# One transpose of 128x32 for the maxima's rows, and the mixer's weights cast on GpSimd from unit 16 on

## The chip, the cores and the metric

The kernel runs on one core of a Trainium2 chip, as one program with one launch. The metric is the device time of one execution in microseconds (us), as the median of several executions; lower is better. The engines of the core are named as in the profile: PE is TensorE (PEld its weight loads), DVE is VectorE, ACT is ScalarE, POOL is GpSimd and SP is SyncE, which here only issues DMAs. Each engine takes its own instructions strictly in the order in which they stand; engines wait for each other by semaphores.

## The reference

All data are float32. The output is `x + s * g`: `s` is full attention with 32 heads of 16 channels over 2048 tokens, `g` is the gate of a token-mixing MLP, and both read the same normalized input.

```python
xn = layernorm(x)                                   # (2048, 512)
# s: attention
q, k, v = split(xn @ wqkv)                          # 32 heads, 16 channels each
p = softmax(einsum("qd,kd->qk", q, k) * 16 ** -0.5) # per head, 2048 x 2048
s = concat(p @ v) @ wo
# g: mixer, the MLP runs over the token axis
u = gelu(einsum("sd,sf->df", layernorm(xn), w1) + b1)   # F = 1792
g = silu(einsum("df,fs->ds", u, w2) + b2).T
out = x + s * g
```

## The kernel before

**Numbers.** A float32 product is made of float32r products: an operand is split into an upper part (a cast to float32r) and a lower part (the rest), and three products are added. `w_split(n)` does that for unit `n` of the mixer's weights, a quarter of a block of 128 columns (512 values a partition): line 179 or 181 casts `raw` to `wh`, on POOL or on ACT, and the helper `sub` (line 107) makes `wl` on POOL. Which engine casts hangs on `steady[0]`, which is set when the loop reaches step 22 (`LEAD`).

**The softmax** is made without a second pass: for each row of queries the maximum of the scores is found first (`max_of`: a score matmul on 48 rows of `q` and `k`, line 537, and a DVE reduction of 128x512, line 541). The negated maxima are then written into two extra rows of the tile `qs[p]` (rows 48 and 49 of each of the two heads in it, upper and lower part), opposite two rows of ones in `ks[p]`. So the second score matmul (`score`, 50 rows, line 1000) gives the score less its maximum, and ACT only has to take the exponential (line 1005). `values` (line 1015) multiplies it with `v`; 32 columns of it are the ones that sum the denominators.

**The main loop** (line 1279) runs over `s` in pairs of steps. A pair has 8 maxima (for the future), 8 scores (22 steps behind), 8 matmuls of `values`, and as many half products of the mixer as a plan by due times gives it (0 to 6, `count`). The order within a pair is written out by hand in strings (`MIDST`). The first 11 pairs, here called the lead, have maxima and the mixer's first products alone; the steady stage follows; the ending (line 1333, strings `ENDING`) has no maxima any more.

**The rows of the maxima.** Sixteen steps of maxima (1024 queries of two heads) make a group; there are 32. At the end of a group, `max_rows` hands out small pieces of work; `piece()` takes one at two places of each pair (all at once in the lead and at the beginning of the ending). Before the change there are five: the reduction to `neg` (128 x 16 values used of 128 x 32), four DVE transposes of 32x32 that each turn one block of 32 partitions into columns of `f` (32 x 128), and with the last of these the cast and the split to `m` on POOL and four DMAs on POOL's own queue, each of which brings eight rows of 128 values into one row of `qs[p]`. The first scores that read these rows stand three pairs after the pair in which the second piece is taken.

**Queues.** All other loads and stores stand on SP, in program order: the mixer's weights (`raw`, three buffers, line 170), the stores of the mixer's inner result (`u_d`), the loads of `q`, `k` and `v`, and at the end the loads and stores of the output's parts. SP's DMAs use eight semaphores in turn, and each waits until the one eight before it has landed.

Of the kernel before, what the change touches and what calls it, by code (L numbers as in the profile page):

```python
# [8 lines left out]
F32 = mybir.dt.float32  # L9
F32R = mybir.dt.float32r  # L10
# [11 lines left out]
def tile_attention_token_mixer(ctx, tc, x, wqkv, wo, w1, b1, w2, b2, out):  # L22
    nc = tc.nc
    P = 128
# [13 lines left out]
    N_BEFORE = 4  # L38
    scale = DH ** -0.5

    def pool(name, bufs, **kw):
        return ctx.enter_context(tc.tile_pool(name=name, bufs=bufs, **kw))
# [63 lines left out]
    def sub(eng, o, a, b):  # L106
        eng.tensor_tensor(out=o, in0=a, in1=b.bitcast(F32), op=OP.subtract)  # L107

    def move(dst, src, queue=nc.sync):

        queue.dma_start(dst.bitcast(F32), src.bitcast(F32))
# [7 lines left out]
    qs, ks, vps = {}, {}, {}  # L119
# [35 lines left out]
    steady = [False]  # L155
# [16 lines left out]
    def w_split(n):  # L172
        if n >= N_W:
            return
        m = quarters[n][2] - quarters[n][1] if n < N_MIX else 4
        whs[n] = wp.tile([P, 4, P], F32R, name="wh")
        wls[n] = wp.tile([P, 4, P], F32R, name="wl")
        if steady[0]:
            nc.gpsimd.tensor_copy(whs[n][:, :m, :], raws[n][:, :m, :])  # L179
        else:  # L180
            nc.scalar.copy(whs[n][:, :m, :], raws[n][:, :m, :])  # L181
        sub(nc.gpsimd, wls[n][:, :m, :], raws[n][:, :m, :], whs[n][:, :m, :])


    with (
# [230 lines left out]
        for c in range(NC):  # L416
# [18 lines left out]
            for n, (part, g) in enumerate(order):  # L435
                m = slice(g * P, (g + 1) * P)
                ps = bank()
                for w, z in ((wh, 0), (wh, 1), (wl, 0)):
                    for kd in range(ND):
                        nc.tensor.matmul(  # L440
                            ps, w[part][:, kd, m], xt[kd][:, z, :],
                            start=w is wh and z == 0 and kd == 0, stop=w is wl and kd == ND - 1,
                        )
                sg = pst.tile([P, 2, 512], F32R, name="sg")
                nc.scalar.copy(sg[:, 0, :], ps)
                sub(nc.vector, sg[:, 1, :], ps, sg[:, 0, :])
                dst = (q_d, k_d)[part][g]
                move(dst[:, :, cs], sg)
                for f in todo[n * per : min((n + 1) * per, cut)]:
                    f()  # L450
                if c == NC - 1 and n == ND - 1:
                    place_qk(0)
                if c == NC - 1 and n == ND:
                    load_qk(0)
                if c == NC - 2 and n == 0:
                    for i in range(3):
                        w_load(i)
                if c == NC - 2 and n == ND:
                    w_split(0)
                    w_load(3)  # L460
                    w_split(1)
                    w_load(4)
                    w_split(2)
# [43 lines left out]
    sm = pool("sm", 2, reuse_waits="tile")  # L507
# [35 lines left out]
    def max_rows(u):  # L543

        p, r = divmod(u // 2, NB)
        span = r // 8
        neg = negs[u // 16 % 2]
        f = sm.tile([32, P], F32, name="f", bufs=1)


        def turned(c):
            nc.vector.transpose(f[:, 32 * c : 32 * c + 32], neg[32 * c : 32 * c + 32, :])  # L552

        def first_():
            nc.vector.tensor_reduce(
                neg[:, :16].rearrange("p (a b) -> p a b", a=2), mxp.pop(u // 16), axis=AX.X, op=OP.max, negate=True,
            )

        def last():
            turned(3)  # L560
            m = sm.tile([16, 2, P], F32R, name="m", bufs=1)
            nc.gpsimd.tensor_copy(m[:, 0, :], f[:16, :])  # L562
            sub(nc.gpsimd, m[:, 1, :], f[:16, :], m[:, 0, :])
            for a in range(2):
                for t in range(2):
                    row = 64 * a + 48 + t
                    move(
                        qs[p][row : row + 1, span * 1024 : (span + 1) * 1024],
                        m[8 * a : 8 * a + 8, t, :], nc.gpsimd,
                    )  # L570

        return first_, *(lambda c=c: turned(c) for c in range(3)), last

# [703 lines left out]
    for s in range(0, total + 1, 2):  # L1279
        t = s - LEAD  # L1280
# [11 lines left out]
        if s < NU and t >= 0:  # L1292
            steady[0] = True
            some = halves(count(s))
            n = len(some)
            of = BEGIN if begun else END if ended[0] else MIDST
            begun = ended[0]
            n = min(x for x in MIDST if x >= n)
# [34 lines left out]
        elif t < NT:  # L1333
# [6 lines left out]
            while any(strings):  # L1340
                for a in range(2):
                    c = strings[a].pop(0) if strings[a] else ""
# [19 lines left out]
        if s < NU and s % 16 == 14:  # L1362
            pieces.extend(max_rows(s + 1))
            piece()
# [5 lines left out]
        if 0 <= t < NT:  # L1370
            p, r = divmod(t, SPP)
# [48 lines left out]
    for k0, kn in parts_:  # L1420
        at = slice(k0 * P, (k0 + kn) * P)
# [53 lines left out]
```

## Time and profile before

| | us |
|---|---|
| median of 3 runs (1633.03 to 1633.38) | 1633.11 |
| the profiled execution | 1634.06 |
| its span, first to last instruction | 1632.2 |
| PE busy in the span | 1621.9 |
| DVE busy | 1418.1 |
| ACT busy | 1194.5 |
| POOL busy | 575.4 |

The lead's first maximum is reduced at 148.7 us, the first score matmul comes at 203 us, the last maximum at 1565 us. A group of the steady stage takes some 44.5 us. A matmul's time is from its start to its modelled end, and two matmuls that use different halves of the rows overlap; so a busy PE may still start its matmuls later than it could, and the distance from start to start is what to look at. Rows of SP are issues of DMAs, not transfers.

### The profile page before, as it was taken

How to read it: one execution, taken by the hardware profiler on the slowest of the kernel's cores; microseconds unless marked ns; L12 is line 12 of the kernel's file. 1: busy time of each engine (PE TensorE's matmuls, PEld its weight loads, DVE VectorE, ACT ScalarE, POOL GpSimd, SP SyncE). 2: the span in 40 equal slices, each digit the busy share in tenths (PEclk: the TensorE clock that was granted, in tenths of full speed). 3: DMA queues.
4: the chain of work that ended last, by engine and by line, in shares of the span. 5: the costliest groups of instructions: out<-in, count | busy, mean ns of one | idle time of the engine just before them, and what ended most of it. 6: DMA issues, size and time to landing. Idle time of an engine off the chain costs nothing.

```text
span 1632.2 us, 31813 instructions
## 1 busy us (share of the span) xinstructions
PE 1621.9 (99%) x11948; PEld 892.0 (55%) x11948; DVE 1418.1 (87%) x2506; ACT 1194.5 (73%) x2297; POOL 575.4 (35%) x676
## 2 busy tenths in 40 slices
PE   9999999999999999999999999999999999999998
PEld 7888845555554545555555545555554545544554
DVE  7655989999999999999999999999999999999955
ACT  4333488777877777787777777787777777788785
POOL 0223743333443334332433223223222332662434
PEclk9999999999999999999999999999999999999999
DMA  6479621415133141836150522305152515354344
GB/s 226 174 247 227 122 59 47 82 34 95 41 53 76 38 79 35 191 121 111 37 85 18 99 57 46 70 30 77 37 85 59 91 37 78 100 110 134 117 151 168
DMA packets 150775, 152.89 MB, mean 94 GB/s; under 512 B 51340, under 2 KB 109708, under 8 KB 147548
## 3 DMA queue, kind: packets, MB, share of 16 engines
q1 hardware_dynamic: 146044, 149.70, 38.8%
q8 instruction: 94, 1.54, 0.4%
q0 software_dynamic: 4288, 0.62, 0.3%
q14 instruction: 61, 0.50, 0.1%
q10 hardware_dynamic: 288, 0.52, 0.1%
HBM read 99.63 MB, written 50.32 MB: 92 GB/s over the span
## 4 chain that ended last, share of the span: by engine, by line
PE 98%; DVE 1%; ACT 0%; DMA 0%; SPq 0%; issue 0%; DVEq 0%; ACTq 0%
PE av L1015 31%; PE sc L1165 16%; PE sc L1000 10%; PE sc L537 8%; PE mx L1000 8%; PE mx L1165 7%; PE mx L537 6%; PE sc L440 3%; PE mx L440 2%; PE mx L1112 1%; PE sc L1112 1%; PE sc L1215 1%; PE av L440 1%; PE sc L116 1%; PE sc L114 1%; PE sc L115 1%
## 5 line engine op out<-in xcount | busy, mean ns | idle before, releaser
L541 DVE TENSOR_REDUCE mxp<-sc 128x1 f32<-128x512 f32 x1129 | 735.9, 681 | 74.7 <-PE sc L537 49.7
L1005 ACT ACTIVATE prob<-sc 128x512 f32<-128x512 f32 x1135 | 638.3, 604 | 168.8 <-PE sc L1000 98.2
L541 DVE TENSOR_REDUCE mxp<-mx 128x1 f32<-128x512 f32 x919 | 606.0, 681 | 50.3 <-PE mx L537 30.9
L1005 ACT ACTIVATE prob<-mx 128x512 f32<-128x512 f32 x913 | 523.1, 606 | 127.3 <-PE mx L1000 71.7
L1015 PE MATMUL av<-prob,vp 128*32 128x512 f32 x4096 | 543.0, 604 | 0.0
L537 PE MATMUL sc<-big 48*128 48x512 f32 x1129 | 427.8, 417 | 0.0
L1000 PE MATMUL sc<-big 50*128 50x512 f32 x1135 | 423.1, 417 | 0.2 <-ACT prob L1005 0.2
L1165 PE MATMUL sc<-hu,wh 64*128 64x512 f32 x1072 | 359.3, 404 | 0.0
L537 PE MATMUL mx<-big 48*128 48x512 f32 x919 | 349.9, 416 | 0.1
L1000 PE MATMUL mx<-big 50*128 50x512 f32 x913 | 346.9, 415 | 0.5 <-ACT prob L1005 0.5
L1000 PEld LDWEIGHTS sc<-big 50*128 50x128 f32 x1135 | 198.2, 185 | 137.9 <-DVE mxp L541 102.0
L537 PEld LDWEIGHTS sc<-big 48*128 48x128 f32 x1129 | 196.9, 185 | 81.7 <-ACT prob L1005 53.5
L1165 PEld LDWEIGHTS sc<-hu,wh 64*128 64x128 f32 x1072 | 193.9, 184 | 58.8 <-issue 41.9
L1000 PEld LDWEIGHTS mx<-big 50*128 50x128 f32 x913 | 162.2, 185 | 107.4 <-DVE mxp L541 83.3
L1165 PE MATMUL sc<-hu,wl 64*128 64x512 f32 x536 | 215.1, 401 | 0.0
L537 PEld LDWEIGHTS mx<-big 48*128 48x128 f32 x919 | 160.9, 185 | 74.4 <-ACT prob L1005 38.1
L1015 PEld LDWEIGHTS av<-prob,vp 128*32 128x32 f32 x4096 | 81.8, 108 | 171.8 <-issue 161.4
L1165 PE MATMUL mx<-hu,wh 64*128 64x512 f32 x464 | 156.2, 405 | 0.0
L179 POOL CAST wh<-raw 128x512 fp32r<-128x512 f32 (+1 forms) x105 | 61.3, 584 | 255.2 <-PE sc L537 57.7
L107 POOL TENSOR_TENSOR wl<-raw,wh 128x512 fp32r<-128x512 f32 (+1 forms) x113 | 136.6, 1210 | 28.9 <-ACT wh L181 20.4
L562 POOL CAST m<-f 16x128 fp32r<-16x128 f32 x32 | 9.0, 280 | 311.2 <-DVE f L552 308.4
L1165 PEld LDWEIGHTS sc<-hu,wl 64*128 64x128 f32 x536 | 98.8, 184 | 13.3 <-issue 5.9
(240 smaller groups left out, 1592.0 us busy)
## 6 DMA issues: line engine op xcount, KB each, us to landing
raw<-in_B_w_dram SPq DMA_DIRECT2D x93, 256.0 KB
big<-k_d SPq DMA_DIRECT2D x96, 128.0 KB
big<-q_d SPq DMA_DIRECT2D x96, 128.0 KB
q_d<-sg SPq DMA_DIRECT2D x16, 512.0 KB
k_d<-sg SPq DMA_DIRECT2D x16, 512.0 KB
num_d<-ev SPq DMA_DIRECT2D x30, 256.0 KB
u_d<-uo SPq DMA_DIRECT2D x14, 512.0 KB
hu<-u_d SPq DMA_DIRECT2D x14, 512.0 KB
```

What stands on the lines that cost most here:

```text
L107: eng.tensor_tensor(out=o, in0=a, in1=b.bitcast(F32), op=OP.subtract)
L114: nc.tensor.matmul(ps, wh, mh, start=first, stop=False)
L115: nc.tensor.matmul(ps, wh, ml, start=False, stop=False)
L179: nc.gpsimd.tensor_copy(whs[n][:, :m, :], raws[n][:, :m, :])
L440: nc.tensor.matmul(ps, w[part][:, kd, m], xt[kd][:, z, :], start=w is wh and z == 0 and kd == 0, stop=w is wl and kd == ND - 1,)
L537: nc.tensor.matmul(ps, q[o : o + 48, r * P : (r + 1) * P], k[o : o + 48, c * 512 : (c + 1) * 512], start=True, stop=True,)
L541: return nc.vector.tensor_reduce(mxp[u // 16][:, a, r % 8, c : c + 1], ps, axis=AX.X, op=OP.max)
L1000: nc.tensor.matmul(ps, ks[p][o : o + 50, kb * P : (kb + 1) * P], qs[p][o : o + 50, at : at + 512], start=True, stop=True,)
L1005: return nc.scalar.activation(e, ps, AF.Exp, scale=scale)
L1015: nc.tensor.matmul(av[32 * j : 32 * j + 32, :], vps[p][:, kbs[c], 16 * a : 16 * a + 32], prob.pop((t, a, c)), start=first, stop=last,)
L1112: nc.tensor.matmul(ps(a), w(r), m(r), start=first, stop=last)
L1165: i = nc.tensor.matmul(ps(), w(r), m(r), start=first and first_half, stop=last and not first_half)
```

## The change

The four transposes become one of 128x32. DVE turns every block of 32x32 in its own partitions, so `f` is now 128 x 32: block `b` of the maxima stays on partitions 32b to 32b+31. `m` is cast and split in this layout (32 values a partition on 128 partitions, before 128 values on 16). A row of `qs[p]` is then gathered from four blocks: four DMAs for each row, 16 in all, each of 8 pieces of 32 values, and they are issued by SP. The group's pieces are now two, so the second, with transpose, cast, split and DMAs, is taken at the place where the first of the four transposes was. Apart from that, `w_split` casts units from 16 on, three of which fall before `steady[0]` is set, on POOL.

```diff
-        if steady[0]:
+        if steady[0] or n >= 4 * N_BEFORE:
             nc.gpsimd.tensor_copy(whs[n][:, :m, :], raws[n][:, :m, :])
         else:
             nc.scalar.copy(whs[n][:, :m, :], raws[n][:, :m, :])
@@ max_rows
-        f = sm.tile([32, P], F32, name="f", bufs=1)
-        def turned(c):
-            nc.vector.transpose(f[:, 32 * c : 32 * c + 32], neg[32 * c : 32 * c + 32, :])
+        f = sm.tile([P, 32], F32, name="f", bufs=1)
...
         def last():
-            turned(3)
-            m = sm.tile([16, 2, P], F32R, name="m", bufs=1)
-            nc.gpsimd.tensor_copy(m[:, 0, :], f[:16, :])
-            sub(nc.gpsimd, m[:, 1, :], f[:16, :], m[:, 0, :])
+            nc.vector.transpose(f, neg)
+            m = sm.tile([P, 2, 32], F32R, name="m", bufs=1)
+            nc.gpsimd.tensor_copy(m[:, 0, :], f)
+            sub(nc.gpsimd, m[:, 1, :], f, m[:, 0, :])
             for a in range(2):
                 for t in range(2):
                     row = 64 * a + 48 + t
-                    move(
-                        qs[p][row : row + 1, span * 1024 : (span + 1) * 1024],
-                        m[8 * a : 8 * a + 8, t, :], nc.gpsimd,
-                    )
-        return first_, *(lambda c=c: turned(c) for c in range(3)), last
+                    to = qs[p][row : row + 1, span * 1024 : (span + 1) * 1024]
+                    to = to.rearrange("o (r g b) -> o r g b", r=8, g=4)
+                    for g in range(4):
+                        at = 32 * g + 8 * a
+                        move(to[:, :, g, :], m[at : at + 8, t, :], nc.sync)
+        return first_, last
```

SP at the end of the lead, before; `u_d` is the store of a mixer block, `raw` a load of weights:

```order
L170 DMA prob<-in_B_w_dram 128x4x128 x2
L111 DMA u_d_104<-uo 128x1024
L170 DMA raw<-in_B_w_dram 128x4x128 x3
L111 DMA u_d_105<-uo 128x1024
L170 DMA raw<-in_B_w_dram 128x4x128 x2
L145 DMA vp<-v_d 128x16x48
```

And now:

```order
L170 DMA prob<-in_B_w_dram 128x4x128 x2
L111 DMA u_d_104<-uo 128x1024
L111 DMA big<-m 1x8x32 x16
L170 DMA raw<-in_B_w_dram 128x4x128 x3
L111 DMA u_d_105<-uo 128x1024
L170 DMA raw<-in_B_w_dram 128x4x128 x2
```

The first group's 16 DMAs stand ahead of the three loads that bring units 16 to 18.

POOL at the same place, from the split of unit 16 on, before:

```order
L107 TENSOR_TENSOR wl<-raw,wh 128x512
L675 TENSOR_TENSOR sq<-sq,u 128x512
L107 TENSOR_TENSOR wl<-raw,wh 128x512
L630 TENSOR_TENSOR u<-u,sq 128x512
L631 TENSOR_TENSOR sq<-u 128x512
L632 TENSOR_SCALAR sq<-sq 128x512
L633 TENSOR_TENSOR sq<-sq,u 128x512
L107 TENSOR_TENSOR wl<-raw,wh 128x512
L678 TENSOR_TENSOR t<-t,u 128x512
```

And now (line numbers are 3 lower):

```order
L179 CAST wh<-raw 128x512
L107 TENSOR_TENSOR wl<-raw,wh 128x512
L672 TENSOR_TENSOR sq<-sq,u 128x512
L179 CAST wh<-raw 128x512
L107 TENSOR_TENSOR wl<-raw,wh 128x512
L627 TENSOR_TENSOR u<-u,sq 128x512
L628 TENSOR_TENSOR sq<-u 128x512
L629 TENSOR_SCALAR sq<-sq 128x512
L630 TENSOR_TENSOR sq<-sq,u 128x512
L179 CAST wh<-raw 128x512
L107 TENSOR_TENSOR wl<-raw,wh 128x512
L675 TENSOR_TENSOR t<-t,u 128x512
```

Three casts were put in ahead of their splits; ACT loses the same three.

SP at the beginning of the ending, now; `u`, `sq`, `xt` and `gt` are buffers for the output's parts (lines 952 and 954 before). Before the change the last two rows below followed directly on `gt`:

```order
L949 DMA u<-g_d 128x512
L951 DMA sq<-y_d 128x512
L949 DMA xt<-g_d 128x512
L951 DMA gt<-y_d 128x512
L111 DMA big<-m 1x8x32 x16
L941 DMA big<-in_A_x_dram 128x512
L927 DMA y_d<-t 128x512
```

The last group's rows stand behind the eight loads that the ending begins with; before they stood on POOL, ahead of the gate's products (lines 922 and 923).

## The prediction

> **What bounds the kernel now.** I read first the busy times and the chain of work that ended last, then DVE's largest groups, then three stretches of one steady group by windows.
>
> ```profile
> PE 1621.9 (99%) x11948; PEld 892.0 (55%) x11948; DVE 1418.1 (87%) x2506; ACT 1194.5 (73%) x2297; POOL 575.4 (35%) x676
> ...
> PE 98%; DVE 1%; ACT 0%; DMA 0%; SPq 0%; issue 0%; DVEq 0%; ACTq 0%
> ...
> L541 DVE TENSOR_REDUCE mxp<-sc 128x1 f32<-128x512 f32 x1129 | 735.9, 681 | 74.7 <-PE sc L537 49.7
> ...
> L541 DVE TENSOR_REDUCE mxp<-mx 128x1 f32<-128x512 f32 x919 | 606.0, 681 | 50.3 <-PE mx L537 30.9
> ```
>
> The chain runs through PE for 98% of the span. DVE, which the change relieves, is well loaded, but in front of its reductions it stood idle for 74.7 + 50.3 = 125 us, most of it until a maximum's matmul was done: an engine that set the pace would not wait so. PE's own 99% says little, since its ends are modelled. So I ask whether PE starts its matmuls more slowly while the transposes run. One group: the reduction to `neg` at 945.43, the four transposes from 946.76 to 954.40, DVE's first idle time ahead of 958.02 (columns of the first rows below: the stretch and its length, then busy us and count by engine).
>
> ```profile
> core 0: us, PE busy (x) PEld busy (x) DVE busy (x) ACT busy (x) POOL busy (x), PEclk, DMA share, GB/s
> 945.30:958.00 12.70, 12.70 (x99) 6.32 (x98) 11.92 (x24) 9.04 (x18) 3.24 (x7) 1.00 0.22 64
> 958.00:972.00 14.00, 14.00 (x110) 7.06 (x108) 12.59 (x21) 10.81 (x21) 3.49 (x5) 1.00 0.16 49
> 972.00:989.70 17.70, 17.70 (x138) 9.22 (x134) 15.94 (x26) 14.73 (x30) 5.58 (x6) 1.00 0.15 46
> ...
> 945.43 0.22 DVE L555 TENSOR_REDUCE neg<-mxp 128x16 f32<-128x64 f32 x1
> ...
> 946.76 0.19 DVE L552 STREAM_TRANSPOSE f<-neg 32x32 f32<-32x32 f32 x1
> ...
> 954.40 0.20 DVE L552 STREAM_TRANSPOSE f<-neg 32x32 f32<-32x32 f32 x1
> ...
> 958.02 1.29 DVE L541 TENSOR_REDUCE mxp<-sc 128x1 f32<-128x512 f32 x2 [0.44 <-PE mx L1165]
> ```
>
> With the transposes PE starts 99/12.70 = 7.80 matmuls per us, without them 110/14.00 = 7.86 and 138/17.70 = 7.80. DVE's share goes from 94% to 90%, and PE hardly notices. PE bounds the steady stage.
>
> **Term 1, DVE in the steady stage.** Three transposes fall away in each of 30 steady groups; the one that stays handles four blocks side by side.
>
> ```profile
> L552 DVE STREAM_TRANSPOSE f<-neg x128: 187/199/204, 188.3 to 1567.5; 32x32 f32<-32x32 f32 x128
> ```
>
> No row shows a transpose of 128x32. Between 0.2 us (one 32x32, if partitions work in parallel) and 0.8 us (four of them), I take 0.2, since other rows of DVE with 128 partitions go by elements per partition. DVE saves 3 x 0.199 = 0.6 us in a group. What reaches PE: had the first stretch run at the rate of the two others together (248/31.70 = 7.82), its 99 matmuls had taken 12.66 us, 0.04 less. Times 30 that is 1.3 us for the whole of neg and transposes (0.22 + 0.80 us of DVE), of which 0.6 us, some 60%, goes: **-0.8 us**. Bounds: 0 (nothing arrives, or the transpose takes 0.8) and -3 (the stretch's loss is twice as large and more, as far as one group can mislead). That all of it arrives is a rival below.
>
> **Term 2, the lead.** Two small gaps of PE stand there.
>
> ```profile
> 188.33 0.84 DVE L552 STREAM_TRANSPOSE f<-neg 32x32 f32<-32x32 f32 x4
> ...
> 189.96 0.39 PE L537 MATMUL sc<-big 48*128 48x512 f32 x1
> 190.40 0.50 PE L537 MATMUL mx<-big 48*128 48x512 f32 x1
> ...
> 204.08 0.63 ACT L181 CAST wh<-raw 128x512 fp32r<-128x512 f32 x1
> ...
> 205.26 0.50 PE L1000 MATMUL mx<-big 50*128 50x512 f32 x1 [0.52 <-ACT prob L1005]
> ```
>
> From 189.96 to 190.40 PE starts nothing for 0.44 us, where it else starts a matmul every 0.23 or so: 0.2 us that DVE's four transposes in a row cost, as I read it. At 205.26 PE waited 0.52 us for an exponential; ahead of the first ones stands the cast of unit 18, which delays them by about 0.5 us and now is POOL's. Both gone: **-0.6 us** (0 to -0.7).
>
> **Term 3, POOL at the end of the lead.** POOL receives three casts and loses four DMAs a group.
>
> ```profile
> L107 POOL TENSOR_TENSOR wl<-raw,wh 128x512 fp32r<-128x512 f32 x97 | 124.9, 1288 | 27.6 <-ACT wh L181 20.4
> L111 POOL DMA_DIRECT2D big<-m x128 | 66.2, 530 | 2.6 <-PE sc L1215 2.6
> L179 POOL CAST wh<-raw 128x512 fp32r<-128x512 f32 x89 | 54.9, 617 | 246.5 <-PE sc L537 56.8 <-PE mx L1000 48.2 <-PE mx L537 47.4
> ...
> 185.06 2.08 SPq L170 DMA_DIRECT2D raw<-in_B_w_dram  x3
> ...
> 965.80 1.09 SPq L730 DMA_DIRECT2D d<-ev  x2
> ...
> 1555.46 0.69 SPq L784 DMA_DIRECT2D uo<-rec_d  x1
> 1562.46 1.28 POOL L791 TENSOR_TENSOR u<-u,uo 96x512 f32<-96x512 f32 x1 [4.89 <-DMA uo<-rec_d]
> ```
>
> The casts cost 3 x 0.62 = 1.9 us, the DMAs of a group 4 x 0.53 = 2.1 us; POOL is ahead, were it not for SP. The loads of units 16 to 18 went out at 185.06; now the 16 small DMAs stand before them, and these wait for `m` (transposed from 188.33, cast and split in some 0.5 us: 189.1). An issue of a small DMA that gathers 256-byte pieces takes 1.09/2 = 0.55 us, the large ones that follow each other 0.43 to 0.47 apart; I take 0.5, bounds 0.34 and 0.55. So the burst takes 8 us, and the loads go out at 197.1 instead of 185.06. Their landing on SP is in no row of mine; between 1.6 us (4 KB on POOL's queue) and 7.0 us (a 512 KB broadcast, 1555.46 to 1562.46) I take 4: unit 16 lands at 201.1, is cast and split by 203.0.
>
> ```profile
> 209.92 1.32 POOL L678 TENSOR_TENSOR t<-t,u 128x512 f32<-128x512 f32 x1
> ...
> 213.04 0.63 ACT L668 CAST uo<-t 128x512 fp32r<-128x512 f32 x1
> ...
> 203.27 0.39 PE L1165 MATMUL sc<-hu,wl 64*128 64x512 f32 x1
> ```
>
> PE's first product with that `wl` stood at 203.27: just in time. Behind it, POOL has ten more instructions up to `t`, now about 10.8 us without a gap, so `t` ends near 213.8 instead of 211.24, and ACT, which is 0.5 us ahead of 213.04 without its cast, waits some 1.3 us with exponentials behind. PE has seven banks and ACT slack of its own: **+0.5 us** (0, if loads land in 2 us; 2.5 if in 6).
>
> **Term 4, the steady rows and the last ones.** In the steady stage the rows must be in place for the score three pairs later.
>
> ```profile
> 955.44 2.08 POOL L111 DMA_DIRECT2D big<-m  x4
> ...
> 960.62 0.19 PEld L1000 LDWEIGHTS sc<-big 50*128 50x128 f32 x1
> ...
> DMA to landing us min/median/max: 1.5/1.6/4.5
> ```
>
> Before: last issue at 957.0, landing 1.6 later, use at 960.62: 2 us to spare. Now `m` is ready at 947.5, the burst lasts until 955.5, lands at 957.1: 3.5 us to spare. SP is held at this place until `m` is there, so loads that it took early now go out with the burst's end; weights are loaded two units (some 25 us) ahead, which covers it: 0.
>
> The ending has less.
>
> ```profile
> 1567.76 0.28 POOL L562 CAST m<-f 16x128 fp32r<-16x128 f32 x1 [2.77 <-DVE one L1227]
> 1568.12 0.52 POOL L107 TENSOR_TENSOR m<-f,m 16x128 fp32r<-16x128 f32 x1
> 1571.27 2.04 POOL L111 DMA_DIRECT2D big<-m  x4 [2.63 <-PE sc L1215]
> 1573.32 1.30 POOL L922 TENSOR_TENSOR t<-t,gt 128x512 f32<-128x512 f32 x1
> 1574.69 1.29 POOL L923 TENSOR_TENSOR t<-t,xt 128x512 f32<-128x512 f32 x1
> ...
> 1570.33 0.32 SPq L954 DMA_DIRECT2D sq<-y_d  x1
> 1576.01 0.32 SPq L952 DMA_DIRECT2D xt<-g_d  x1
> 1576.38 0.42 SPq L954 DMA_DIRECT2D gt<-y_d  x1
> ...
> 1578.80 0.50 PE L1000 MATMUL mx<-big 50*128 50x512 f32 x1
> ```
>
> The rows' first use is at 1578.80. The burst stands behind `xt` and `gt`, and `xt` waits for POOL's L923 (1575.98 before). Without its DMAs POOL comes to L922 at 1567.8 and ends L923 at 1570.4; so SP issues `xt` and `gt` until 1571.25, then the burst. Its last DMA goes out 15 x 0.5 later, 1578.75, lands 1.6 later at 1580.4: PE stands for **+1.6 us**. Bounds: 0 (issues of 0.34: landing at 1577.9) and +5.2 (0.55 and a landing of 4.5 behind the 256 KB loads: 1584.0). PE is the chain there, nothing takes it back.
>
> The Trainium skill, "DMA: Bandwidth & Descriptors", section "Anatomy of one DMA — SWDGE (gpsimd) path", gives a DMA a fixed cost of about 2.0 us; this trace has 1.6 for the nearest, so the measurement is used. By the page the estimate of this stall would be 2.0 and the sum +1.1.
>
> **Sum**: -0.8 - 0.6 + 0.5 + 1.6 = +0.7 us. On the profiled execution (1634.06; span 1632.2 and 1.9 around it) that is 1634.8; this execution lay 0.95 above the median of the runs, 1633.11, so the predicted median is **1633.8**.
>
> **Rivals.** *DVE sets the pace around each group's end.* For it: DVE is 94% busy in 945.3 to 958. Then all of 3 x 0.199 x 30 = 17.9 us arrives, 1615; a quarter of it, 4.5 us, gives 1629.4 with the other terms. Against it: the even rates of PE and DVE's 125 us of idle. 0.14 for a gain over 0.2%.
> *SP's burst decides, slower.* Place: the ending, where eight loads of 256 KB go ahead of it. From landing at 1578.8 on each us counts one for one; at the upper bounds +5.2, with the lead's 2.5 and nothing gained about 1641, typically 1638. For it: `xt` did wait 5.7 us here. Should an issue take over 0.72 us, the steady rows come late too (947.5 + 16 x 0.72 + 1.6 = 960.6), and 0.8 would cost 30 x 1.3 = 39 us, 1672; SP's rows are all against that. Together 0.22.
> The Trainium skill, same page, section "Specifications", speaks against pieces under 512 bytes (read-modify-write); here they are 128, before 512. No row prices it.
> *The wide transpose costs as much as four.* Then term 1 and 0.2 of term 2 fall away: +1.7, 1634.8; 0.06, no change either. My forecast has 0.58.
>
> **The numbers.** A measurement of this kernel tells about 0.2% (3.3 us) from no change: faster is under 1629.8, slower over 1636.4. Faster 0.14, same 0.58 + 0.06 = 0.64, slower 0.22. Range: terms at their low ends with the first rival's edge give 1629.4, with the second rival's typical 1638: 1629 to 1638.5.
>
> **What would show it.** Term 1: a transpose of 0.2 us, DVE's idle ahead of L541 up by about the 18 us saved, with PE's steady rate unchanged. Term 2: no wait near 205 us. Term 3: units 16 to 18 loaded near 197 us, POOL's `wl` near 203. Term 4: 16 issues of 0.5 us on SP, and in the ending PE held at its first score of the last group. Wrong it would be if steady groups became shorter than 44.4 us, or if the ending showed no gap.

## The result, and the profile after

| | before | after |
|---|---|---|
| median, us | 1633.24 (1633.03 to 1634.18, 4 runs) | 1656.40 (1654.44 to 1659.94, 4 runs) |
| the profiled execution, us | 1634.06 | 1654.44 |
| its span, us | 1632.2 | 1652.7 |

The ratio is 1.0143, 95% interval 1.0125 to 1.0161. The change makes the kernel 23 us slower; 1633.8 was predicted, and the range ended at 1638.5. The profiled execution lies 2.0 us under the median, so the traces have 20.4 of the 23 us to account for.

From the page of the profile after: the busy times, the chain by engine, DVE's two largest groups (busy, mean ns of one, idle before them).

```profile
PE 1627.6 (98%) x11948; PEld 891.6 (54%) x11948; DVE 1407.9 (85%) x2410; ACT 1194.0 (72%) x2294; POOL 505.0 (31%) x551
...
PE 89%; DMA 4%; SPq 3%; POOL 2%; DVE 1%; issue 1%; ACT 0%; DVEq 0%; POOLq 0%
...
L541 DVE TENSOR_REDUCE mxp<-sc 128x1 f32<-128x512 f32 x1129 | 739.2, 684 | 90.0 <-PE sc L537 60.6
...
L541 DVE TENSOR_REDUCE mxp<-mx 128x1 f32<-128x512 f32 x919 | 608.4, 684 | 61.1 <-PE mx L537 37.2
```

And from the groups by line and form, the transposes:

```profile
L556 DVE STREAM_TRANSPOSE f<-neg 128x32 f32<-128x32 f32 x32 | 6.5, 202 | 0.1
```

The transposes did what was asked of them: 25.3 us of DVE became 6.5, and DVE's idle time ahead of its reductions rose from 125 to 151 us. New is the chain: it ran through PE for 98% of the span, now for 89%. The rest goes through DMAs, SP's queue and POOL.

The waits of PE that the change brought (total us, times, longest):

```profile
PE mx L997 <- DMA big<-m: 8.2, 3, 5.7
...
PE sc L997 <- DMA big<-m: 3.7, 2, 2.4
PE sc L997 <- ACT prob L1002: 2.2, 1, 2.2
```

And the 512 DMAs with the rows of the maxima, from the view of the tile `m` (duration of an issue in ns: least, median, most; first and last start):

```profile
L111 SPq DMA_DIRECT2D big<-m x512: 634/635/798, 188.4 to 1595.6; - x171
```

An issue takes 0.635 us (the median). The places themselves, from the timeline after (start, length, engine, what; in brackets what was waited for and how long): SP's burst, then the first score that reads its rows. In order of time: the end of the lead, groups 11 and 16, then group 17 as an ordinary one (the weight load is that of its first score), groups 24, 27 (burst alone) and 28, the ending.

```profile
188.36 11.12 SPq L111 DMA_DIRECT2D big<-m  x16
199.53 1.54 SPq L170 DMA_DIRECT2D raw<-in_B_w_dram  x3
...
202.70 0.61 POOL L179 CAST wh<-raw 128x512 fp32r<-128x512 f32 x1 [6.14 <-DMA raw<-in_B_w_dram]
203.37 0.50 PE L1162 MATMUL sc<-hu,wh 64*128 64x512 f32 x1 [1.03 <-POOL wh L179]
...
685.28 11.00 SPq L111 DMA_DIRECT2D big<-m  x16
...
697.66 0.47 PE L997 MATMUL mx<-big 50*128 50x512 f32 x1 [1.46 <-DMA big<-m]
...
906.36 13.60 SPq L111 DMA_DIRECT2D big<-m  x16
...
921.33 0.46 PE L997 MATMUL mx<-big 50*128 50x512 f32 x1 [1.04 <-DMA big<-m]
...
952.44 11.00 SPq L111 DMA_DIRECT2D big<-m  x16
...
965.79 0.19 PEld L997 LDWEIGHTS sc<-big 50*128 50x128 f32 x1
...
1263.37 13.90 SPq L111 DMA_DIRECT2D big<-m  x16
...
1278.53 0.46 PE L997 MATMUL sc<-big 50*128 50x512 f32 x1 [1.24 <-DMA big<-m]
...
1398.98 11.00 SPq L111 DMA_DIRECT2D big<-m  x16
...
1447.02 11.08 SPq L111 DMA_DIRECT2D big<-m  x16
...
1459.59 0.76 PE L997 MATMUL sc<-big 50*128 50x512 f32 x1 [2.44 <-DMA big<-m]
...
1584.85 11.37 SPq L111 DMA_DIRECT2D big<-m  x16
...
1597.49 0.76 PE L997 MATMUL mx<-big 50*128 50x512 f32 x1 [5.66 <-DMA big<-m]
```

Sixteen issues take 11.0 us, 0.69 from start to start. In the ordinary group the last one starts 0.635 us before the burst's end, at 962.8, and a landing takes 1.67 us (next fence); so the rows are there at 964.5, 1.3 us before their first use at 965.79. At four of the 30 steady groups (11, 16, 24 and 28) and in the ending the burst starts late or is held up within itself, and this 1.3 us is not enough.

Why it is late there, from the chain of the groups at 906 and at 1447:

```profile
905.20 8.65 DMA raw<-in_B_w_dram
...
913.88 0.63 SPq L111
...
919.32 1.67 DMA big<-m
...
921.33 0.46 PE mx L997
...
1414.56 12.71 DMA raw<-in_A_wo_dram
...
1446.83 0.15 POOL m L558
```

At 906 the burst stops halfway: SP's DMAs use eight semaphores in turn, and one of the 16 had to wait until a 256 KB load, issued at 905.20, was in place. Group 24's burst of 13.9 us stands behind the same sequence of loads. At 1447 it is `m` that is late: the burst of group 27 (1398.98 to 1409.99) put off six loads of 256 and 512 KB and, behind them, a block of the output weights; that was issued at 1414.56 and took 12.71 us to land, POOL stood for it, and POOL's products that it delayed stand ahead of `m`. At 685 SP itself was late, with large loads still to issue when `m` was ready (682.3); in the ending its burst began 4.1 us behind `m` (1580.75) for the same reason.

A long wait cost more than itself. Windows of the trace after: behind the end of group 28's wait and right after that, then the same for the ending (columns as in the prediction; PEclk is the granted clock of TensorE as a share of full speed).

```profile
core 0: us, PE busy (x) PEld busy (x) DVE busy (x) ACT busy (x) POOL busy (x), PEclk, DMA share, GB/s
1459.60:1465.60 6.00, 6.00 (x27) 2.05 (x27) 2.29 (x4) 2.77 (x5) 0.00 (x0) 0.50 0.72 229
1466.00:1472.00 6.00, 6.00 (x48) 3.15 (x46) 4.88 (x8) 4.62 (x9) 2.57 (x2) 1.00 0.55 115
1597.50:1602.10 4.60, 4.60 (x21) 2.68 (x25) 0.12 (x2) 3.81 (x8) 0.00 (x0) 0.50 0.58 168
1602.50:1607.10 4.60, 4.60 (x38) 2.24 (x34) 1.66 (x7) 3.26 (x7) 0.00 (x0) 1.00 0.27 101
```

In these two waits (2.44 and 5.66 us) the granted clock fell to 0.50 and stayed there for 6.8 us, and PE got through 27 matmuls in 6.0 us, where it then did 48. With the waits of 1.0 to 2.2 us elsewhere in this trace it stayed at 1.00. By the starts of the same matmuls in the traces before and after, group 28 lost 2.8 us in the wait and 2.8 more under the low clock, the ending 6.2 and 1.8: 4.6 us of the 20.4 come from the clock. No run varies the clock alone, but in the traces of all runs here it fell, while PE still had work, only in or just behind a wait of 1.6 us or more, and with every wait of 2.4 us or more.

To see how much each stretch lost, I compare the starts of the same instruction in two traces: the difference is taken at the first reduction of pair 7 (before the first rows), of pair 16 (behind the lead's end), of the last pair, and at the end of the span. For all kernels of this study, in us against the profile before:

| kernel | up to pair 7 | lead's end, pairs 7 to 16 | steady, pair 16 to last | ending | span |
|---|---|---|---|---|---|
| the change | -0.5 | +2.9 | +9.8 | +8.1 | +20.4 |
| rows on POOL | -0.8 | +3.1 | -0.9 | +1.3 | +2.7 |
| cast alone | -0.8 | -0.5 | -0.4 | 0.0 | -1.6 |
| rows alone | +0.4 | +1.4 | +12.7 | +7.8 | +22.3 |
| four on SP | -0.1 | 0.0 | -0.8 | +0.8 | -0.1 |
| shared queues | +0.7 | -0.9 | -1.1 | +6.2 | +4.9 |
| some groups on POOL | +0.3 | +3.1 | +7.4 | +3.9 | +14.6 |
| twenty on SP, repeated | -0.5 | +11.4 | +256.6 | +15.4 | +282.8 |
| double transposes | -0.4 | +1.0 | +12.6 | 0.0 | +13.2 |
| shared, last as before | -1.0 | -0.9 | -0.9 | -0.6 | -3.4 |
| half dose of transposes | 0.0 | +0.5 | +1.5 | 0.0 | +2.0 |
| shared in six groups | -0.4 | -0.9 | -1.0 | +2.1 | -0.2 |
| four spare on SP | -0.3 | +6.9 | +58.0 | +9.5 | +74.0 |

The first column is scatter, since nothing is changed up to there: up to 1 us between two executions. So a difference of less than 1 us elsewhere in this table proves nothing by itself.

### The profile page after: what moved, and what is told of

Its sections match the earlier page's. It is cut to its first block, busy times and chain, and to the rows that moved or that the text cites. A ratio compares the mean times of both kernels' runs of the same rounds, so it can differ in the third digit from the quotient of the medians.

```text
span 1652.7 us, 32191 instructions
## 1 busy us (share of the span) xinstructions
PE 1627.6 (98%) x11948; PEld 891.6 (54%) x11948; DVE 1407.9 (85%) x2410; ACT 1194.0 (72%) x2294; POOL 505.0 (31%) x551
## 4 chain that ended last, share of the span: by engine, by line
PE 89%; DMA 4%; SPq 3%; POOL 2%; DVE 1%; issue 1%; ACT 0%; DVEq 0%; POOLq 0%
PE av L1012 28%; PE sc L1162 14%; PE sc L997 9%; PE mx L997 7%; PE sc L537 7%; PE mx L1162 6%; PE mx L537 6%; PE sc L440 3%; SPq L111 3%; PE mx L440 2%; PE sc L1109 1%; DMA raw<-in_A_wo_dram 1%; DMA raw<-in_B_w_dram 1%; PE av L440 1%; DVE mxp L541 1%
## 5 line engine op out<-in xcount | busy, mean ns | idle before, releaser
L179 POOL CAST wh<-raw 128x512 fp32r<-128x512 f32 x108 | 62.8, 582 | 446.3 <-PE sc L1162 156.7
L1162 PEld LDWEIGHTS mx<-hu,wh 64*128 64x128 f32 x464 | 83.8, 184 | 26.6 <-issue 20.1
```

Source lines behind the costliest of these rows:

```text
L1162: i = nc.tensor.matmul(ps(), w(r), m(r), start=first and first_half, stop=last and not first_half)
```

## The experiments

Theory A: the 20 us come from the length of SP's burst, 11 us in which nothing else goes out there and behind which the rows themselves come late. A ratio is always to runs of the kernel before that were taken together with the run (medians 1633.32 to 1634.01 us). Rivals: the small pieces are slow on any queue (B); the moved casts cost the lead (C); SP's standing at the burst until `m` is there costs, not the length (D).

**Rows on POOL.** The change with the 16 DMAs on POOL's queue.

```diff
-                        move(to[:, :, g, :], m[at : at + 8, t, :], nc.sync)
+                        move(to[:, :, g, :], m[at : at + 8, t, :], nc.gpsimd)
```

> The changed kernel with the 16 small DMAs of a group on GpSimd's queue instead of SyncE's; the single transpose and the moved casts stay. Theory A (SyncE's burst costs the 20 us: 16 x 0.69 us = 11.1 us in which nothing else can be issued there, and which itself stands behind whatever SyncE is held at): the waits of PE for the rows at 697.7, 921.3, 1278.5 and 1459.6 us go, since GpSimd's burst of 16 x 0.53 = 8.5 us starts as soon as m is there; the ending keeps a small loss, as 8.5 us instead of 2.1 stand ahead of GpSimd's products there (0 to 6). Time 1633 to 1639. Theory B (pieces of 128 bytes and four times the DMAs are slow to land, whatever the queue): the waits stay, 1650 or more. Theory C (the three casts moved to GpSimd cost the 2.4 us at the end of the lead): the gap at 203 us stays at 1 us or more, the others go.

Measured: 1637.65 us, ratio 1.0029 (1.0018 to 1.0040). B is out: the same pieces of 128 bytes cost nothing in the steady stage (-0.9). Its loss sits in the lead. From its timeline on POOL:

```profile
188.34 8.04 POOL L111 DMA_DIRECT2D big<-m  x16
196.40 1.27 POOL L107 TENSOR_TENSOR wl<-prob,wh 128x512 fp32r<-128x512 f32 x1
```

From its waits of PE, and then from the view of the tile `m` (on POOL the trace tells the time to landing too: least, median, most):

```profile
PE mx L1109 <- POOL wl L107: 2.0, 2, 1.8
```

```profile
DMA to landing us min/median/max: 1.5/1.6/7.5
```

POOL is held for 8.0 us, and the `wl` behind it, which PE's mixer products need, comes late. It is the same fault on another queue.

**Cast alone.** The kernel before with `or n >= 4 * N_BEFORE` added to the condition in `w_split`, nothing else.

> The kernel before with the second part of the change alone: units 16 to 18 cast on GpSimd; four transposes and four DMAs on GpSimd stay. Theories A and B: their loads go out near 185 us as before, the casts end before 203 us, and the 0.5 us wait of PE at 205 us goes: 1632.5 to 1633.4. Theory C: a new gap of PE near 203 us, 1635 to 1636.

Measured: 1633.30 us, ratio 0.9999 (0.9989 to 1.0008). The casts by themselves change nothing that can be measured.

**Rows alone.** The change with the old condition, `if steady[0]:`.

> The change without its second part: units 16 to 18 are cast on ScalarE as before; one transpose and 16 DMAs on SyncE stay. Theories A and B: the loads of these units still go out near 199.5 us, behind the burst, and the cast on ScalarE waits for them with exponentials behind it: the lead loses as much as with the change or up to 2 us more, 1655 to 1659. Theory C: the lead's 2.4 us come back, 1652 to 1654.

Measured: 1658.11 us, ratio 1.0153 (1.0138 to 1.0168). So the rows alone cost everything, as A expected, and the casts' price (C) does not show in the total. One thing C had right: the lead's end loses 1.4 us here and 2.9 with the casts on POOL. When the loads are late, POOL has more queued behind them than ACT; the wait of 2.2 us for an exponential, which stands behind POOL's late `t`, is 0.2 us here.

**Four on SP.** The kernel before with its four DMAs of 512-byte pieces on SP.

```diff
-                        m[8 * a : 8 * a + 8, t, :], nc.gpsimd,
+                        m[8 * a : 8 * a + 8, t, :], nc.sync,
```

> The kernel before (four transposes, the rows of 512 bytes, four DMAs) with these four DMAs on SyncE instead of GpSimd. It tells the length of the burst from the holding of SyncE at its first DMA. Theory A with the length deciding: 4 x 0.69 = 2.8 us from 955.4 us on in the group shown, in place by 959.4 with the use at 960.6; hardly a wait in the steady rows, 0 to 1 us in the ending: 1633 to 1636. Theory A with the holding deciding (SyncE stands until m is there, and what it took early before now goes out late): the waits in the four groups with large loads and in the ending stay for the greater part, 1640 to 1650. Theory B (size of the pieces): 1633.

Measured: 1634.22 us, ratio 1.0006 (0.9996 to 1.0016). Its DMAs in the view of the tile `m`, and their burst in the group of the prediction, from the timeline:

```profile
L111 SPq DMA_DIRECT2D big<-m x128: 634/642/789, 189.4 to 1575.2; - x128
```

```profile
954.40 2.82 SPq L111 DMA_DIRECT2D big<-m  x4
```

D is out for this length: SP stands at the first of four DMAs in each group, and nothing is lost. An issue with pieces of 512 bytes takes as long as one with pieces of 128: with eight pieces in each, it is the number of DMAs that counts and not their bytes.

**Shared queues.** The change with eight of the 16 on SP and eight on POOL.

```diff
-                        move(to[:, :, g, :], m[at : at + 8, t, :], nc.sync)
+                        move(to[:, :, g, :], m[at : at + 8, t, :], nc.sync if g < 2 else nc.gpsimd)
```

> The changed kernel with its 16 small DMAs shared out: the eight of blocks 0 and 1 on SyncE, the eight of blocks 2 and 3 on GpSimd. SyncE's burst is halved to 8 x 0.69 = 5.5 us, GpSimd's is 8 x 0.51 = 4.1 us. Theory A (length of the burst on SyncE): the four waits of PE in the steady stage (1.5, 1.0, 1.2 and 2.4 us) are shorter than the 5.5 us gained and go; the end of the lead gets its loads near 194 instead of 199.5 us, gap there under 0.5 us; the ending loses 7.8 - 5.5 = 2.3 us. 1633.5 to 1637. Theory D (what counts is that SyncE stands at the burst's first DMA until m is there, not how long the burst is): the four waits stay by more than half, 1645 to 1650.

Measured: 1637.61 us, ratio 1.0022 (1.0013 to 1.0032), just over the 1637 that A allowed. Theory A holds: the lead and the steady stage are where they were before the change, the ending loses 6.2 us. There SP's half still stands behind eight large loads (the last of them and the half, from the timeline; then PE's wait, and one of SP's):

```profile
1574.25 0.42 SPq L951 DMA_DIRECT2D gt<-y_d  x1
1574.72 5.49 SPq L111 DMA_DIRECT2D big<-m  x8
```

```profile
PE mx L997 <- DMA big<-m: 3.1, 1, 3.1
```

```profile
SPq L949 <- POOL t L920: 3.0, 1, 3.0
```

The ending was expected to lose 2.3. Not reckoned with was that the loads ahead of SP's half wait for a product of POOL (L920), which POOL's half now puts off, nor the clock: it is at 0.50 behind the wait of 3.1 us, and 2.4 of the 6.2 us are lost there.

**Some groups on POOL.** The change with the 16 on POOL in groups 0, 11, 16, 24, 27 and 31, on SP in the others.

```diff
-                        move(to[:, :, g, :], m[at : at + 8, t, :], nc.sync)
+                        move(to[:, :, g, :], m[at : at + 8, t, :], nc.gpsimd if u // 16 in (0, 11, 16, 24, 27, 31) else nc.sync)
```

> The changed kernel with the 16 DMAs on GpSimd in six groups only (0 in the lead, 11, 16, 24, 27 and the last, 31), on SyncE in all others, group 28 among them. Group 28 lost most in the steady stage (5.5 us: m ready at 1447.3 instead of 1442.9, since GpSimd stood until 1427.3 for a block of the output weights which SyncE issued at 1414.6, behind the burst of group 27). Theory A: the 24 other groups cost nothing though their bursts take 11 us on SyncE, and group 28 heals too with its own burst still on SyncE, because 27's is not before the weights. Left are the lead's 2.3 and the ending's 1 as with all on GpSimd: 1635 to 1638. Theory E (group 28's own burst on SyncE is what costs): its 5.5 us stay, 1641 to 1644.

Measured: 1647.84 us (1644.83 to 1650.75), ratio 1.0085 (1.0070 to 1.0100). That is above both expectations. Groups 11, 16 and 24 healed, 28 did not (6.4 us, 2.4 of them under the low clock), so my account of it was not the whole. From the timeline of this kernel around group 28, and one piece of its chain:

```profile
1396.93 8.24 POOL L111 DMA_DIRECT2D big<-m  x16
...
1407.18 0.65 SPq L777 DMA_DIRECT2D u<-num_d  x1
...
1444.48 0.21 POOL L558 CAST m<-f 128x32 fp32r<-128x32 f32 x1
```

```profile
1417.03 8.79 DMA raw<-in_A_wo_dram
```

On POOL the burst of group 27 puts off POOL's own products by 8.2 us; SP's next loads wait for the buffers that these read, and the block of output weights is late again. So, as I read it, `m` is late whichever queue takes all of 27's burst, and then 28's burst of 11 us is too long. The ending's +3.9, most of it behind the last product with `v`, I can't explain; this kernel also scatters most.

**Twenty on SP, repeated.** The four DMAs of block 3 issued twice.

```diff
-                    for g in range(4):
+                    for g in (0, 1, 2, 3, 3):
```

> The changed kernel with the four DMAs of block 3 issued twice (same data): 20 instead of 16 on SyncE, 13.8 instead of 11.0 us. It measures how near the other groups are to the edge. In group 17 of the changed kernel the last DMA is issued at 962.8 us, lands 1.66 later at 964.5, and the first score that reads it loads its weights at 965.8: 1.3 us to spare. Theory A: 4 x 0.69 = 2.75 us more turn this into 1.4 us of wait in each of some 25 groups (35 us), and the five late places lose 2.75 each (14 us): 1656 + 49 = 1705, 1690 to 1715. Theory F (the steady groups have slack beyond the row's own landing, only the places with large loads are late): 1656 + 14 = 1670, up to 1675.

Measured: 1916.76 us, ratio 1.1727 (1.1710 to 1.1745), far over both numbers. The dose was another than I meant to give. One burst in the timeline, and a piece of it in the chain:

```profile
1199.21 17.76 SPq L111 DMA_DIRECT2D big<-m  x20
```

```profile
1205.13 0.64 SPq L111
1205.82 1.66 DMA big<-m
1207.49 0.63 SPq L111
```

In this program a second write to the same place waits until the first has landed, four times in a burst: 17.8 us instead of 13.8. Every ordinary group then has a gap of PE of 4 to 7 us, and behind each the granted clock falls to 0.50 (its mean over the span is 0.931, before 0.998). The burst is 6.8 us longer than with the change, and most of that is waited for, which speaks against F; the next run is the cleaner one.

**Four spare on SP.** The same dose without that wait: one more DMA behind each four, into a tile that is not read.

```diff
+            spare = sm.tile([1, 2, 512], F32R, name="spare", bufs=1)
...
                     for g in range(4):
                         at = 32 * g + 8 * a
                         move(to[:, :, g, :], m[at : at + 8, t, :], nc.sync)
+                    at = 96 + 8 * a
+                    move(spare[:, t, 256 * a : 256 * a + 256], m[at : at + 8, t, :], nc.sync)
```

> The changed kernel with four more DMAs of the same form on SyncE behind the others of a group, writing into a tile that nobody reads, so that none waits for another's landing. The burst is 20 x 0.69 = 13.8 us, but the rows' own 16 DMAs are interleaved with the spare ones, and the last one of them goes out behind 18 of the 20. Theory A with a margin of 1.3 us in an ordinary group: about 2 x 0.69 to 3 x 0.69 = 1.4 to 2.1 us later, of which 0.1 to 0.8 us are waited for in each of some 25 groups (2 to 20 us), and the late places lose 2 us each (14 us): 1672 to 1692. Theory F (no ordinary group is near its edge): the late places alone, 1666 to 1672.

Measured: 1706.78 us, ratio 1.0447 (1.0431 to 1.0463), above both expectations; F is out. The rows' last DMA goes out 3 x 0.69 = 2.1 us later. Seven ordinary groups in a row (17 to 23, from one reduction to `neg` to the next) take 45.43 us each instead of 44.44: they lose 1.0 us, so the margin was 1.1 us, near the 1.3 read above. Over the 24 ordinary groups it is some 21 us of the 74. The lead and groups 11, 16, 24 and 28 lose 4 to 5 us more than with the change, twice what I gave them, and groups 5 and 29 become late ones (6.1 and 3.3 us); there the estimate failed. One reason is the clock, which I had not reckoned with: it falls to 0.50 behind the waits of all these places, and at group 11, for one, 1.6 of the 4.1 us were lost behind the wait.

**Shared in six groups.** The change with the 16 shared between the two queues in groups 0, 11, 16, 24, 27 and 28, on POOL in group 31, and on SP in the 25 others.

```diff
+    def at_queue(n, g):
+        return nc.gpsimd if n == 31 or (n in (0, 11, 16, 24, 27, 28) and g > 1) else nc.sync
...
-                        move(to[:, :, g, :], m[at : at + 8, t, :], nc.sync)
+                        move(to[:, :, g, :], m[at : at + 8, t, :], at_queue(u // 16, g))
```

> The changed kernel with the 16 DMAs shared between SyncE and GpSimd in six groups only (0, 11, 16, 24, 27 and 28), all on GpSimd in the last group, and all on SyncE in the other 25, whose bursts still take 11 us. Theory A (the loss sits in those places alone): lead and steady within 1.5 us of before, the ending +1: 1633 to 1636. Theory G (the 25 others lose a little each which the gaps do not show): 1638 or more.

Measured: 1633.41 us, ratio 1.0000 (0.9991 to 1.0009). This is the strongest run for theory A: 25 bursts of 11 us on SP cost nothing, and the whole 23 us sat in the seven places that were altered, within the 1 us that a stretch scatters by.

**Double transposes, and half the dose.** The kernel before with each of its four transposes done twice, and with two of the four done twice.

```diff
         def turned(c):
-            nc.vector.transpose(f[:, 32 * c : 32 * c + 32], neg[32 * c : 32 * c + 32, :])
+            for _ in range(2):      # half the dose: range(2 if c in (0, 2) else 1)
+                nc.vector.transpose(f[:, 32 * c : 32 * c + 32], neg[32 * c : 32 * c + 32, :])
```

> The kernel before with each of its four transposes of a group done twice: 4 x 0.199 x 30 = 24 us more on VectorE in the steady stage, nothing else changed. It is the opposite of what the change takes from VectorE. My forecast's rate (some 0.03 us of PE per 0.4 us of VectorE): +1.5 us at most, 1633.2 to 1635. Rival theory R1 (VectorE sets the pace around a group's end, all of it arrives): 1650 to 1657.

> The kernel before with two of the four transposes of a group done twice (blocks 0 and 2): 0.4 us more on VectorE per group, half of the dose that cost 0.42 us of the 0.80 per group. Theory K (a knee: VectorE has about 0.38 us of slack around a group's end; beyond it each us arrives whole): 0 to 0.1 us per group, 1633.5 to 1636.5. Theory P (a fixed share of 53% of VectorE's time arrives, whatever the dose): 0.21 us per group, 6.4 us, about 1640; then the saving of 0.6 us should have brought something too.

Measured: 1647.79 us, ratio 1.0086 (1.0070 to 1.0103), and 1635.54 us, ratio 1.0014 (1.0005 to 1.0023). The first lies between my number and R1's: I had reckoned with one rate for both directions. Per group (median from `neg` to `neg`): 44.43 us before, 44.47 with 0.4 us more on DVE, 44.82 with 0.8 us more. So it is a knee (theory K): most of the first 0.4 us is absorbed, and of the 0.4 us on top 0.35 arrives. The stretch of the prediction, in the kernel with double transposes:

```profile
core 0: us, PE busy (x) PEld busy (x) DVE busy (x) ACT busy (x) POOL busy (x), PEclk, DMA share, GB/s
952.13:964.83 12.70, 12.70 (x96) 5.87 (x96) 12.44 (x28) 9.05 (x18) 2.74 (x7) 1.00 0.21 64
```

DVE is busy for 12.44 of 12.70 us, before 11.92; PE starts 96 matmuls instead of 99.

**Shared queues, last group as before.** Eight and eight in all groups but the last, whose rows are made by the old function (four transposes, four DMAs on POOL).

```diff
-            pieces.extend(max_rows(s + 1))
+            pieces.extend((max_rows_last if s // 16 == NU // 16 - 1 else max_rows)(s + 1))
```

> The changed kernel with its 16 DMAs shared between SyncE (8) and GpSimd (8) as in the split of the queues, and with the last group's rows made as in the kernel before (four transposes of 32x32, four DMAs on GpSimd). The split lost nothing outside the ending (its shift against before was -1.0 us at the last group) and 5 us there. Theory A: the ending is that of before again, so -1 to 0 us: 1632.3 to 1633.6, no measurable gain since VectorE's saved 18 us do not reach TensorE. Rival (VectorE's saving was there all along and SyncE hid it): under 1630.

Measured: 1630.65 us (1630.28 to 1631.73), ratio 0.9984 (0.9976 to 0.9993). It beats the kernel before by 2.7 us or 0.16%; it lies below my 1632.3 and above the rival's 1630. Which part brings the 2.7 us isn't separated; its profile has less than 1 us in each stretch, the stretch in which nothing is changed included. How SP waits in it, beside the same row of the change (us, times, longest):

```profile
SPq L111 <- POOL m L107: 306.3, 30, 23.2
```

```profile
SPq L111 <- POOL m L107: 306.5, 30, 23.2
```

SP stands just as long for `m` in the kernel that wins as in the one that loses 23 us. The standing was never the cost.

## Why the prediction was wrong

**The step that failed** is the price of an issue in terms 3 and 4: "I take 0.5, bounds 0.34 and 0.55". Measured: 0.635, 0.69 from start to start, and so 11.0 us for the burst instead of 8. The upper bound came from a small copy on SP (`d<-ev`, pieces of 256 bytes), and these 16 cost more; why isn't shown. The prediction's own lines had an issue of 0.69 us on SP (`uo<-rec_d` at 1555.46), which the bounds left out. The price moves the prediction's own sums by 16 x 0.19 = 3 us at each place where the burst's end counts, the lead and the ending: at most some 1640. In the steady stage it did more than the sums could say: a burst 3 us shorter would, by estimate, have spared all four waits there (1.0 to 2.4 us), but by the prediction's rule, under 0.72 an issue costs these rows nothing. So **a second step failed**, the "0" for the steady rows (below), and a third thing was not in the sum at all: the granted clock of 0.50 behind the two longest waits, 4.6 us.

**Term 1, DVE: right, and small.** The transpose of 128x32 takes 0.202 us, as taken. In the kernels that don't lose rows the steady stage is 0.9 to 1.1 us shorter where -0.8 was forecast; since the cast alone shows -0.4 there and four on SP -0.8, most of that may be scatter. The knee fits that: before the change DVE was just off the edge, so that 0.6 us less brings next to nothing, while 0.8 us more costs 0.39 a group. "PE bounds the steady stage" was right; the rival that DVE sets the pace falls.

**Term 2, the lead's gaps: as forecast, within the scatter.** With the cast alone the lead's end is 0.5 us shorter, with both parts and the lead's burst shared 0.9 in three kernels alike; -0.6 was forecast. The wait of 0.52 us near 205 is gone with the cast alone. But 0.9 us is no more than the scatter of a stretch, so this agrees and proves little.

**Term 3, the end of the lead: mechanism right, size off.** Loads behind the burst, then late casts, then ACT waiting for `t` with exponentials behind: all of it is there, with 2.9 us net instead of +0.5 - 0.6. The loads went out at 199.53 instead of 197.1, and the cast of unit 16 began at 202.70, where 201.1 was reckoned.

**Term 4, steady rows: "0" was wrong in four of 30 groups**, and these cost +10.7 of the 20.4 us, 2.8 of it under the low clock (9.8 for the whole stage, since the other groups gained). The sentence that failed is "weights are loaded two units (some 25 us) ahead, which covers it: 0". It asks whether what stands behind the burst comes late. I didn't ask what the burst itself stands behind, nor that DMAs behind one another share eight semaphores, so that a small copy waits for a large load to land. The other 26 groups do keep their rows in time, those looked at (17 to 23) with some 1.1 to 1.3 us to spare and not the 3.5 I reckoned.

**Term 4, ending: mechanism right as far as it went, size off**: PE held at the first score of the last group, for 5.7 us, and 8.1 us in all where +1.6 was forecast. The price of an issue makes 16 x 0.19 = 3 us of the difference; the burst started at 1584.85, which less the 12.3 us of shift up to there is 1572.6, 1.3 later than my 1571.25. Together 1.6 + 3 + 1.3 = 5.9, near the wait. Behind it the clock of 0.50 cost 1.8 us more, which "PE is the chain there" did not reckon with.

**The rival that came true** is the burst on SP, and my price for it, 1638, was too low: I had the ending and the lead in it, and for the steady stage only the case in which every group is late ("over 0.72 us"). At 0.69 it was some that were late. "SP's rows are all against that" was too strong: they did not show this transfer, and one of them stood at 0.69. The range ended too low for the same reason: its upper bound came from the same price. Its lower end has a slip that changes nothing here: 1629.4 takes term 1's 0.8 us twice, and 1630.1 would be the sum; and `xt`, said to wait 5.7 us, waited 5.3.

Of the rules on small copies: pieces of 128 bytes on POOL landed in 1.6 us (median) in these runs, as those of 512 did before. The Trainium skill, "DMA: Bandwidth & Descriptors", section "Specifications", warns of pieces under 512 bytes, which this trace doesn't bear out for copies within the core's memory; the same page, section "Why small descriptors are slow (HBM only)", says that such copies don't suffer, and there the trace agrees.

An issue took 0.69 us here against 1.67 to land, so 16 in a row are the larger part, and sharing them between two queues took 1656.40 to 1637.61 us. The Trainium skill, same page, section "Issuing engines are not separate DMA queues", says that issuing on several engines saves only the time of initiating, usually small beside the DMA itself. That it is this time which is saved agrees with the runs; that it is small does not, for a burst of small copies.

## What to carry to other kernels

Price a moved DMA by issues of its own form on its new queue; if the trace has only something near it, the bounds must take in every issue that the queue shows, and the burst is count times price. Then ask twice for each burst: what stands behind it, and what it stands behind, place by place and not for the typical group alone, since a margin of 1 us holds in 26 groups and breaks in four. Look at the granted clock behind every long wait of PE: the time lost there is not in any row of waits. An engine that is 94% busy off the critical path may be worth nothing when relieved and cost nearly in full when loaded a little more.

## What the runs showed of the hardware

- A small copy within the core's memory took 0.635 to 0.642 us to issue on SP, for 8 pieces of 128 or of 512 bytes alike, and 0.50 us on POOL (16 in 8.04); loads of 256 KB took 0.32 to 0.42 us on SP in the rows of the ending, and another large load (`uo<-rec_d`) 0.69 us.
- DVE's transpose of 128x32 took 0.202 us, one of 32x32 0.199.
- A DMA that the program let wait for an earlier one's landing held its whole queue until then: 1.66 us for a small copy in the kernel with repeated DMAs.
- The granted clock of TensorE fell to 0.50 with waits of PE of 2.44 and 5.66 us in the kernel after, for 6.8 us each time (from 1458.8 and from 1595.3), and not with waits of 1.03 to 2.21 us.
